# Extra TensorE matmuls with unread results in the drain and between the experts, and one group's slot products moved later

## The chip, the core and the metric

The kernel runs on one core of a Trainium2 chip. The metric is the device time of one execution in microseconds (us); smaller is better. Each execution also has a span, from its first to its last recorded instruction. In the fast executions of this study the time is 1.7 to 2.2 us above the span, mostly 1.8, so a span can be turned into a time by adding about 1.8 us.

## The reference, cut to what matters

Two steps. First a gated recurrence over 5056 positions of 4 sequences, 256 channels wide:

```python
f = lower_bound + (1.0 - lower_bound) * sigmoid(f_logit)
h = f[:, t] * h + (1.0 - f[:, t]) * x[:, t]      # for each t in order
```

Then a soft mixture of experts over all 20224 tokens: 32 slots, 4 for each of 8 experts.

```python
logits = x @ phi                       # 20224 x 32
d = softmax(logits over tokens);  slot_input = d.T @ x
slot_out[e] = relu(slot_input[e] @ w1[e]) @ w2[e]     # w1: 256x1024, w2: 1024x256
out = softmax(logits over slots) @ slot_out
```

No slot input is complete before the last token is scanned, and no output row can be written before the slot outputs are complete. So the kernel has three stages: loading and scanning, a short middle that is mostly matmuls (the drain of the last group, then the experts), and writing the output.

Of the kernel before, what the change touches and what calls it, by code (L numbers as in the profile page):

```python
# [18 lines left out]
def kernel(  # L19
# [10 lines left out]
    nc = tc.nc  # L30
# [5 lines left out]
    P = 128  # L36
# [3 lines left out]
    G = P * R  # L40
    n_grp = (S + G - 1) // G
    n_unit = n_grp * B
# [58 lines left out]
    w1_sb = [store.tile([P, DC, F], BF16, name=f"w1_sb{e}") for e in range(E)]  # L101
    w2_sb = [store.tile([P, FC, D], BF16, name=f"w2_sb{e}") for e in range(E)]

    def load_w(i):
        if i < E:
            nc.gpsimd.dma_start(out=w1_sb[i], in_=w1_r[i])
        else:
            k = FC // 2 if i == 2 * E - 1 else FC
            for c in range(0, FC, k):
                nc.gpsimd.dma_start(out=w2_sb[i - E][:, ds(c, k)],  # L110
                                    in_=w2_r[i - E][:, ds(c, k)])


    W_AT = {12: 1, 18: 1, 24: 1, 30: 1, 34: 3, 35: 1, 36: 8}
    w_next = [0]
# [5 lines left out]
    with tc.tile_pool(name="ld", bufs=3) as ld, \  # L121
# [141 lines left out]
        def row_sums(g):  # L263
            n_p = rows(g)
            ew = etall[:, ds(g * G, n_p * R)].rearrange("s (p r) -> s p r", r=R)
            for r in range(R):
                nc.tensor.matmul(rs_ps[:n_p, g, r], ew[:, :, r], ones,
                                 start=True, stop=True, skip_group_check=True)

        def slots(g):  # L270
            n_p = rows(g)
            et, ht = ets.pop(g), hts.pop(g)
            for r in range(R):
                for b in range(B):
                    nc.tensor.matmul(slot_ps[ds(b * NS, NS), :], et[:n_p, r, b],  # L275
                                     ht[:n_p, b, r],
                                     start=(g == 0 and r == 0),
                                     stop=(g == n_grp - 1 and r == R - 1),
                                     skip_group_check=True)

        def unit(f, m):
            if 0 <= m < n_unit:
                f(m)
# [19 lines left out]
        def late_weights(bs, copy):  # L303
            k, w = ds(bs[0] * NS, len(bs) * NS), len(bs) * NS
            ew = etall[k, ds(last * G, G)].rearrange("s (p r) -> s p r", r=R)
            if bs[0] == 0:
                ets[last] = etok.tile([P, R, B, NS], BF16, name="et", tag="et")
            for r in range(R):
                nc.tensor.transpose(late_ps[:, r, k], ew[:, :, r], ident[k, k])
            copy(ets[last][:, :, ds(bs[0], len(bs))].rearrange("p r b s -> p r (b s)"),  # L310
                 late_ps[:, :, k])

        def late_slots(bs):
            for r in range(R):
                for b in bs:
                    nc.tensor.matmul(slot_ps[ds(b * NS, NS), :], ets[last][:, r, b],
                                     hts[last][:, b, r],
                                     start=False, stop=r == R - 1,
                                     skip_group_check=True)
# [19 lines left out]
        for n in range(n_unit):  # L339
            if n < SINGLE - 2:  # L340
                if n:
                    unit(u_to_channels, n + 1)
                    unit(to_tokens, n - 1)
                s_to_channels(n + 2)
                decay(n + 2, 1)
                if n + 3 < SINGLE:
                    gate(n + 3, 1)
                else:
                    gate(n + 3)
                if n % 2 == 0:  # L350
                    unit(load, n + AHEAD)
                unit(enter, n + 3)
            else:
                if n % 2 == 0:
                    unit(load, n + AHEAD)
                    unit(gate, n + 4)
                else:
                    unit(decay, n + 1)
                if n == 34:
                    exps(7)  # L360
                elif n != 33:
                    group(exps, n - 2)

                unit(enter, n + 3)
                for _ in range(W_AT.get(n, 0)):
                    load_w(w_next[0])
                    w_next[0] += 1

                unit(to_tokens, n - 1)
                if n % 2 == 0:  # L370
                    unit(s_to_channels, n + 2)
                    unit(s_to_channels, n + 3)
                unit(u_to_channels, n + 1)
                group(logits, n - 1)
            if n == n_unit - 1:
                tail = psp.tile([P, 2, G], F32, name="tail", tag="sp")
                rs_ps = tail[:, 0, ds(0, n_grp * R * B)].rearrange(
                    "p (g r b) -> p g r b", r=R, b=B)
                late_ps = tail[:, 1].bitcast(BF16)[:, ds(0, R * P)].rearrange(
                    "p (r s) -> p r s", r=R)  # L380
                logits(last, [0, 1, 2])
                late_exps([0, 1, 2])
                for g in range(4):
                    row_sums(g)

            unit(scan, n)
            if n == 0:
                rep_constants()
            unit(keep_tokens, n - 1)
            if n == 35:  # L390
                weights_to_tokens(7)
            elif n != 34:
                group(weights_to_tokens, n - 3)
            if n == 36:
                slots(6)
            elif n == 37:
                slots(7)
            elif n != 35:
                batch(slots, n - 4, 0)
                batch(slots, n - 4, 1)  # L400
        late_weights([0, 1, 2], nc.scalar.copy)
        logits(last, [3])
        late_exps([3])
        to_tokens(n_unit - 1)
        nc.vector.tensor_copy(hts[last][:, B - 1].rearrange("p r d -> p (r d)").bitcast(F32),
                              hps.pop(n_unit - 1).rearrange("p r c -> p (r c)"))
        late_slots([0, 1, 2])
        late_weights([3], nc.vector.tensor_copy)
        late_slots([3])
        for g in range(4, n_grp):  # L410
            row_sums(g)
# [3 lines left out]
    with tc.tile_pool(name="ew", bufs=1) as ew, \  # L415
# [12 lines left out]
        for o in range(DC):  # L428
            nc.tensor.matmul(sin_ps[:, o], slot_v[:, o], rep2[:, :NS],
                             start=True, stop=True, skip_group_check=True)  # L430
        sin = ew.tile([P, DC, NS], BF16, name="sin")
        for o in range(DC):
            nc.vector.tensor_scalar_mul(sin[:, o], sin_ps[:, o], omlb[:, ds(o, 1)])
# [23 lines left out]
            his.append(hi)  # L457
        cs_ps = pm.tile([P, 1], F32, name="cs_ps", tag="pm")
        nc.tensor.matmul(cs_ps, rep2, cs1, start=True, stop=True)
        for q in range(E // Q):  # L460
            ht_ps = psu.tile([P, FC, P], BF16, name="ht_ps", tag="up")
            hi_v = his[q].rearrange("p (c f) -> p f c", f=FC)
            for fc in range(FC):
                nc.tensor.transpose(ht_ps[:, fc], hi_v[:, fc], ident)

            src = ht_ps.rearrange("p f (j s) -> p f j s", s=NS)[:, :, :, ds(0, SPE)]
            src = bass.AP(tensor=src.tensor, offset=src.offset + q * Q * SPE,
                          ap=[list(src.ap[0]), [P, FC], [NS + SPE, Q], [1, SPE]])
            dst = hid[:, :, ds(q * Q, Q), ds(0, SPE)]
            dst = bass.AP(tensor=dst.tensor, offset=dst.offset + q * Q * SPE,  # L470
                          ap=[list(dst.ap[0]), [E * NS, FC], [NS + SPE, Q], [1, SPE]])
            if q == 0:
                nc.scalar.copy(dst, src)
            else:
                nc.vector.tensor_copy(dst, src)
            for w in range(W):
                e = E - W + w
                if e // Q == q:
                    src = ht_ps[:, :, ds((e % Q) * NS + e * SPE, SPE)]
                    nc.scalar.copy(wide[:, :, w, :, ds(e * SPE, SPE)],  # L480
                                   src.unsqueeze(2).broadcast_to([P, FC, B, SPE]))
# [8 lines left out]
        for e in range(E - W):  # L490
            for fc in range(FC):
                nc.tensor.matmul(so4_ps[ds(fc % 4 * NS, NS), :], hid[:, fc, e],
                                 w2_sb[e][:, fc],
                                 start=(e == 0 and fc < 4),
                                 stop=(e == E - W - 1 and fc >= FC - 4),
                                 skip_group_check=True)
        so4 = ew.tile([P, D], F32, name="so4")
        nc.vector.tensor_copy(so4, so4_ps)
        so_ps = pm.tile([P, D], F32, name="so_ps", tag="pm")
        nc.tensor.matmul(so_ps, rep2, so4, start=True, stop=False, skip_group_check=True)  # L500
        for w in range(W):
            for fc in range(FC):
                nc.tensor.matmul(so_ps, wide[:, fc, w].rearrange("p b s -> p (b s)"),
                                 w2_sb[E - W + w][:, fc],
                                 start=False, stop=w == W - 1 and fc == FC - 1,
                                 skip_group_check=True)
# [73 lines left out]
```

## The kernel before: what the change touches

The tokens are cut into 10 groups of 512 positions times 4 sequences, so there are 40 units; group 9 is the last. In each unit VectorE scans and TensorE transposes. The end of the main loop and the drain, cut:

```python
for n in range(n_unit):
    # ... loads, gates, transposes, logits of earlier groups ...
    if n == n_unit - 1:
        tail = psp.tile([P, 2, G], F32, name="tail", tag="sp")
        # rs_ps is a view of tail[:, 0], late_ps one of tail[:, 1]
        logits(last, [0, 1, 2])
        late_exps([0, 1, 2])
        for g in range(4):
            row_sums(g)
    unit(scan, n)
    unit(keep_tokens, n - 1)
    # ... weights_to_tokens; slot products of the groups 6 and 7 at n = 36, 37 ...
    elif n != 35:
        batch(slots, n - 4, 0)      # at n = 39: group 8
        batch(slots, n - 4, 1)
late_weights([0, 1, 2], nc.scalar.copy)
logits(last, [3])
late_exps([3])
to_tokens(n_unit - 1)
# ... copy ...
late_slots([0, 1, 2])
late_weights([3], nc.vector.tensor_copy)
late_slots([3])
for g in range(4, n_grp):
    row_sums(g)
nc.vector.tensor_copy(slot_sb, slot_ps)
```

The experts, cut. The tile names in the profiles are `sin_ps` (slot inputs), `hi_ps` (first layer), `ht_ps` (hidden, transposed) and `so_ps` (second layer). Six experts go through `hid`; the last two go through `wide`.

```python
sin_ps   = ...  4 matmuls          # slot inputs, then a VectorE multiply
hi_ps    = ... 32 matmuls with w1  # four experts side by side in the array
ht_ps    = ... 2 x 8 transposes
so4_ps   = ... 48 matmuls with w2 of the experts 0 to 5
so_ps    = rep2 x so4              # gathers the six
so_ps   += 16 matmuls, wide x w2 of the experts 6 and 7
slot_out = so_ps * rcs
```

The weights come through GpSimd's DMA queue, converted to bf16, in this order: the eight w1, then the eight w2. The last w2 comes in two halves:

```python
def load_w(i):
    if i < E:
        nc.gpsimd.dma_start(out=w1_sb[i], in_=w1_r[i])
    else:
        k = FC // 2 if i == 2 * E - 1 else FC
        for c in range(0, FC, k):
            nc.gpsimd.dma_start(out=w2_sb[i - E][:, ds(c, k)], in_=w2_r[i - E][:, ds(c, k)])
```

The softmax here doesn't subtract the row's maximum and nothing guards it: scores larger than these inputs give would overflow.

## Time and profile before

| | us |
|---|---|
| time, median of 3 (range) | 209.4 (209.04 to 209.43) |
| the profiled execution: span | 208.8 |
| the profiled execution: time | 210.53 |

From the page of the kernel before: its span, then the granted TensorE clock in tenths of full speed and the busy share of the DMA engines in tenths, in 40 slices of 5.2 us each.

```profile
span 208.8 us, 3060 instructions
...
PEclk9999859999999979997999969586975555555555
DMA  5999999999999999999999999999069999999994
```

DMA is full in nearly every slice but the 29th and 30th (146 to 157 us): the end of the middle stage. The clock falls to 5 tenths in parts of the middle.

The same kernel, busy time of each engine in stretches of 5 us; the last three columns are the granted clock (1.00 is full), the DMA share and GB/s.

```profile
core 0: us, PE busy (x) PEld busy (x) DVE busy (x) ACT busy (x) POOL busy (x), PEclk, DMA share, GB/s
...
130.00:135.00 5.00, 4.77 (x48) 2.24 (x48) 3.34 (x5) 1.16 (x3) 3.58 (x3) 0.55 1.05 212
135.00:140.00 5.00, 4.62 (x53) 3.30 (x52) 1.34 (x3) 0.79 (x2) 0.00 (x0) 0.77 1.07 214
140.00:145.00 5.00, 4.50 (x43) 2.02 (x44) 1.86 (x5) 1.19 (x2) 0.00 (x0) 0.66 1.05 194
145.00:150.00 5.00, 4.46 (x75) 3.64 (x74) 1.76 (x6) 0.70 (x3) 0.00 (x0) 1.00 0.29 54
```

TensorE is busy over 4.4 us of each 5, at a clock of 0.55 to 0.77 until 145 us. DMA, meanwhile, is also full until about 145 us: these are the weights.

The same kernel's TensorE in order of time. The columns are start, duration, engine, line, operation, output and inputs, sizes, count, and in brackets the idle time before and what ended it.

```profile
130.23 0.99 PE L210 MATMUL hp<-ident_f,h 128*128 128x128 f32 x4 [0.90 <-DVE h L199]
131.15 1.04 PE L234 MATMUL lg<-h,phi 128*32 128x512 bf16 x6
...
132.75 1.04 PE L275 MATMUL slot_ps<-ht,et 112*32 112x256 bf16 x16
...
134.16 1.03 PE L234 MATMUL lg<-h,phi 128*32 128x512 bf16 x2
...
138.39 1.22 PE L267 MATMUL tail<-ones,etall 128*128 128x4 bf16 x24
...
140.61 3.53 PE L449 MATMUL hi_ps<-w_sb,sin 128*32 128x512 bf16 x32 [0.50 <-DVE sin L433]
...
148.20 1.91 PE L503 MATMUL so_ps<-w_sb,wide 128*128 128x256 bf16 x16
```

The slot products of group 8 (132.75) stand ahead of the last logits (134.16). The first layer takes 3.53 us, nearly all at half clock. The last 16 matmuls run without a wait.

The same kernel's chain of waits at the end of the middle stage: start, duration, engine, what.

```profile
148.36 1.76 PE so_ps L503 x16
150.15 0.49 DVE slot_out L507
150.68 0.78 PE op L520 x16
```

In this execution no transfer stands in the chain: from 130.2 us on TensorE, with short VectorE steps between, leads to `slot_out`.

### The profile page before, as it was taken

How to read it: one execution, taken by the hardware profiler on the slowest of the kernel's cores; microseconds unless marked ns; L12 is line 12 of the kernel's file. 1: busy time of each engine (PE TensorE's matmuls, PEld its weight loads, DVE VectorE, ACT ScalarE, POOL GpSimd, SP SyncE). 2: the span in 40 equal slices, each digit the busy share in tenths (PEclk: the TensorE clock that was granted, in tenths of full speed). 3: DMA queues.
4: the chain of work that ended last, by engine and by line, in shares of the span. 5: the costliest groups of instructions: out<-in, count | busy, mean ns of one | idle time of the engine just before them, and what ended most of it. 6: DMA issues, size and time to landing. Idle time of an engine off the chain costs nothing.

```text
span 208.8 us, 3060 instructions
## 1 busy us (share of the span) xinstructions
PE 136.6 (65%) x1084; PEld 94.8 (45%) x1084; DVE 146.2 (70%) x160; ACT 133.9 (64%) x180; POOL 98.1 (47%) x66
## 2 busy tenths in 40 slices
PE   0657567675867597747867296989757677877400
PEld 0336445564655475546656285455533233343100
DVE  1677539999999979999799589533385364655520
ACT  3575798899999988899885964302083445456320
POOL 1555669966998396938979892500000000000000
PEclk9999859999999979997999969586975555555555
DMA  5999999999999999999999999999069999999994
GB/s 196 415 412 408 411 410 406 411 411 408 397 321 421 345 384 414 407 318 414 411 345 373 189 213 213 214 213 191 10 249 397 407 407 406 407 407 405 337 376 177
DMA packets 19982, 71.26 MB, mean 341 GB/s; under 512 B 2240, under 2 KB 2240, under 8 KB 19968
## 3 DMA queue, kind: packets, MB, share of 16 engines
q1 hardware_dynamic: 17232, 62.66, 76.0%
q0 software_dynamic: 2448, 8.39, 20.5%
q8 instruction: 8, 0.13, 0.2%
q10 hardware_dynamic: 288, 0.03, 0.1%
q14 instruction: 6, 0.05, 0.1%
HBM read 58.75 MB, written 20.71 MB: 381 GB/s over the span
## 4 chain that ended last, share of the span: by engine, by line
PE 25%; DMA 23%; DVE 22%; ACT 11%; issue 8%; SPq 3%; POOL 3%; DVEq 0%; ACTq 0%; POOLq 0%
DMA out_dram<-ob 13%; DVE h L199 13%; DMA f_t<-in_f_logit_dram 10%; PE hp L210 7%; ACT s_t L151 5%; DVE ob L527 5%; PE sp L167 5%; PE up L167 3%; DVE ht L219 3%; POOL u_t L162 3%; SPq L549 3%; ACT a L189 2%; ACT ob L533 2%; PE lg L234 2%; PE hi_ps L449 2%
## 5 line engine op out<-in xcount | busy, mean ns | idle before, releaser
L162 POOL TENSOR_TENSOR u_t<-s_t,x_t 128x1024 bf16<-128x1024 bf16 x39 | 83.0, 2154 | 26.0 <-ACT s_t L151 23.1
L199 DVE TENSOR_TENSOR_SCAN h<-a,h,up 128x512 bf16<-128x512 f32 (+1 forms) x72 | 86.1, 1249 | 6.4 <-ACT ht L219 3.4
L210 PE MATMUL hp<-ident_f,h 128*128 128x128 f32 (+1 forms) x160 | 32.0, 328 | 31.3 <-DVE ht L219 17.8
L189 ACT ACTIVATE a<-sp,nomlb 128x1024 f32<-128x1024 bf16 (+2 forms) x46 | 43.4, 995 | 11.3 <-PE sp L167 8.7
L527 DVE TENSOR_TENSOR ob<-op,rrow 128x1024 f32<-128x1024 f32 (+2 forms) x25 | 28.9, 1180 | 21.1 <-DMA out_dram<-ob 17.8
L151 ACT ACTIVATE s_t<-f_t 128x2048 bf16<-128x2048 f32 (+1 forms) x23 | 38.8, 1690 | 6.7 <-DMA f_t<-in_f_logit_dram 6.4
L533 ACT ACTIVATE ob<-op,rrow 128x256 f32<-128x256 f32 (+1 forms) x64 | 25.0, 477 | 28.0 <-DVE ob L527 19.3
L210 PEld LDWEIGHTS hp<-ident_f,h 128*128 128x128 f32 (+1 forms) x160 | 23.4, 209 | 41.8 <-DVE ht L219 21.4
L520 PE MATMUL op<-slot_out,etall 32*128 32x256 bf16 (+1 forms) x160 | 33.0, 379 | 12.6 <-ACT ob L533 10.2
L167 PE MATMUL sp<-ident_f,s_t 128*128 128x128 f32 x160 | 26.4, 315 | 9.6 <-ACT s_t L151 8.5
L167 PE MATMUL up<-ident_f,u_t 128*128 128x128 f32 x160 | 26.6, 292 | 4.2 <-POOL u_t L162 4.1
L520 PEld LDWEIGHTS <-etall 32*128 32x128 bf16 (+1 forms) x160 | 15.2, 130 | 30.3 <-issue 25.9
L167 PEld LDWEIGHTS sp<-ident_f,s_t 128*128 128x128 f32 x160 | 22.5, 167 | 11.0 <-issue 5.8
L167 PEld LDWEIGHTS up<-ident_f,u_t 128*128 128x128 f32 x160 | 20.1, 151 | 6.3 <-POOL u_t L162 5.5
L219 DVE COPY ht<-hp 128x512 f32<-128x512 f32 (+1 forms) x20 | 13.5, 674 | 6.7 <-PE hp L210 6.7
L219 ACT COPY ht<-hp 128x512 f32<-128x512 f32 (+1 forms) x19 | 11.1, 582 | 4.3 <-PE hp L210 4.3
L199 DVE TENSOR_TENSOR_SCAN h<-a,up 128x512 bf16<-128x512 f32 x8 | 9.2, 1205 | 1.2 <-PE up L167 1.2
L234 PE MATMUL lg<-h,phi 128*32 128x512 bf16 (+1 forms) x80 | 8.1, 431 | 0.0
L275 PE MATMUL slot_ps<-ht,et 128*32 128x256 bf16 (+1 forms) x144 | 6.7, 315 | 0.0
L110 POOL DMA_DIRECT2D w_sb<-in_moe_w_dram x9 | 4.8, 558 | 3.7 <-DMA w_sb<-in_moe_w_dram 3.7
L151 ACT ACT_TABLE_LOAD x4 | 5.1, 1283 | 1.7 <-PEq L564 1.7
L454 ACT ACTIVATE hi<-hi_ps 128x512 bf16<-128x512 f32 x2 | 1.2, 597 | 6.8 <-issue 5.7
(62 smaller groups left out, 72.2 us busy)
## 6 DMA issues: line engine op xcount, KB each, us to landing
x_t<-in_x_dram SPq DMA_DIRECT2D x40, 512.0 KB, 10.2
f_t<-in_f_logit_dram SPq DMA_DIRECT2D x17, 1024.0 KB, 12.0
out_dram<-ob SPq DMA_DIRECT2D x34, 512.0 KB, 6.0
w_sb<-in_moe_w_dram POOLq DMA_DIRECT2D x15, 512.0 KB, 9.0
f_t<-in_f_logit_dram SPq DMA_DIRECT2D x6, 512.0 KB, 7.9
out_dram<-ob SPq DMA_DIRECT2D x4, 448.0 KB, 6.5
out_dram<-ob SPq DMA_DIRECT2D x4, 256.0 KB, 2.3
w_sb<-in_moe_w_dram POOLq DMA_DIRECT2D x2, 256.0 KB, 19.4
```

Source lines behind the costliest of these rows:

```text
L151: nc.scalar.activation(sts[n // 2][:, ds(n % 2, k)], fs[n // 2][:, ds(n % 2, k)], ACT.Sigmoid, scale=-1.0)
L162: nc.gpsimd.tensor_tensor(uts[n], s_t, x_t, ALU.mult)
L167: nc.tensor.transpose(ps[:, :, r], t[:, r], ident_f)
L189: nc.scalar.activation(decays[n // 2, o][:, ds(n % 2, k), :T], sp[:, ds(n % 2, k), :T, o], ACT.Identity, scale=nomlb[:, ds(o, 1)], bias=1.0)
L199: nc.vector.tensor_tensor_scan(h[:, :T, o], decays[n // 2, o][:, n % 2, :T], up[:, :T, o], hs[n - B][:, ds(used(n // B - 1) - 1, 1), o] if ...
L210: nc.tensor.transpose(hp[:n_p, r], hw[:, :n_p, r], ident_f)
L219: copy(hts[g][:n_p, b].rearrange("p r d -> p (r d)").bitcast(F32), hps.pop(n)[:n_p].rearrange("p r c -> p (r c)"))
L234: nc.tensor.matmul(lg[ds(b * NS, NS), :], phi[:, o], hs[g * B + b][:, :T, o], start=o == 0, stop=o == DC - 1, skip_group_check=True)
L275: nc.tensor.matmul(slot_ps[ds(b * NS, NS), :], et[:n_p, r, b], ht[:n_p, b, r], start=(g == 0 and r == 0), stop=(g == n_grp - 1 and r == R ...
L520: nc.tensor.matmul(op[:n_p, r], ew[ds(b * NS, NS), :, r], slot_out[ds(b * NS, NS), :], start=True, stop=True, skip_group_check=True)
L527: nc.vector.tensor_tensor(ob[:n_p, ds(r, k)], op[:n_p, ds(r, k)], rrow[:n_p, g, ds(r, k), ds(b, 1)].broadcast_to([n_p, k, D]), ALU.mult)
L533: nc.scalar.activation(ob[:n_p, r], op[:n_p, r], ACT.Copy, scale=rrow[:n_p, g, r, ds(b, 1)])
```

## The change

The intent is to keep TensorE's clock up. The change puts matmuls whose results nobody reads ("spins", 128x512, bf16) where TensorE is thought to wait, and puts useful work, group 8's slot products, into the wait after the last logits. There are 27 spins. The diff, with the unchanged lines cut:

```diff
+    def spin(dst, k):
+        for _ in range(k):
+            nc.tensor.matmul(dst, w1_sb[0][:, 0, :P], w1_sb[0][:, 0, :G],
+                             start=True, stop=True, skip_group_check=True)
 ...
                 for g in range(4):
                     row_sums(g)
-
+                late_weights([0, 1, 2], nc.scalar.copy)
+                spin(lgs[0][:, ds(G, G)], 2)
+
+            if n in (n_unit - 3, n_unit - 2):
+                spin(lgs[0][:, ds(G, G)], 3)
             unit(scan, n)
 ...
-            elif n != 35:
+            elif n != 35 and n != n_unit - 1:
                 batch(slots, n - 4, 0)
                 batch(slots, n - 4, 1)
-        late_weights([0, 1, 2], nc.scalar.copy)
         logits(last, [3])
 ...
-        late_slots([0, 1, 2])
+        late_slots([0, 1])
         late_weights([3], nc.vector.tensor_copy)
+        slots(last - 1)
+        late_slots([2])
         late_slots([3])
 ... after the slot inputs:
+        spin(tail[:, 1], 3)
 ... ahead of the hidden transposes, and after each of their two halves:
+        spin(tail[:, 1], 2)
+            spin(tail[:, 1], 2)
 ... after the second layer of the experts 0 to 5:
+        spin(tail[:, 1], 2)
 ... ahead of the second layer of the experts 6 and 7:
+        spin(tail[:, 1], 8)
```

## The prediction

> **What bounds the kernel now.** By the page's slices and the busy-by-stretch view: loading and scanning (0 to 127 us, DMA share near 1.0), the drain and experts (127 to 152 us), the output (152 to 209 us, DMA share 1.0, about 405 GB/s). The change acts in the middle one. There the chain of waits runs almost wholly through TensorE from 130.2 to 150.1 us, whose waits are short: 0.9, 0.7, 0.6, 0.5, 0.5 and 0.4 us. By the clock record TensorE is at 0.5 from 130.5 to 137.3 and from 140.7 to 144.1 us, else at 1.0.
>
> [...] all changes lie whole multiples of 3.41 us apart.[...]
>
> **What it costs and gives.** 27 extra 128x512 matmuls; from the first-layer products (0.85 us for eight, four at a time, at half clock) I estimate 0.43 us each at half and 0.22 at full clock.
> - 3+3 before the scans of units 37 and 38 fill idle time at 126.5 and delay the last weight transposes by 0.65 us, to about when VectorE is ready for its copy (130.0). If they hold the clock, the half-clock stretch 130.5 to 137.3 goes.
> - Group 8's 16 slot matmuls (1.04 us) leave the path ahead of the last logits and fill the wait for the last weights' copy (0.4 us idle). Two spins (0.4 to 0.85) take their old place.[...]
> - First layer: 3.5 us at half, about 1.8 at full clock.
> - Against it: the spins around the hidden transposes stand where TensorE did not wait (about 1.3 us), and the eight before the last two experts cost 1.7 us.
>
> **What limits the gain.** The weight queue. By the packets of the software queue the last half of the last weight lands at 147.9 us; its four matmuls (0.119 us each) can end at 148.5 at best, against 150.1 now: at most 1.6 us can be won. All at full clock, I get the eight spins ending about 147.3 and the last expert at 149.2: gain 0.9 us. If the clock still falls at 137.3[...], half-clock spins make it about 0.5 us slower. The output is bound by DMA, so either passes one to one to the end.
>
> **Prediction: 208.7 us, 80% range 207.9 to 209.6.** Faster by over 2%: 1%. Within 2%: 98%. Slower: 1%.
>
> **What would show it.** Clock record: 1.0 from 124 past 134 us; the dip at 141 to 144 gone or shorter. Timeline: last logits about 133 instead of 134.2; late row sums starting about 136 instead of 138.4; first layer 1.8 to 2.5 us; second layer starting before 145; eight spins of 1.7 us; slot_out 0.5 to 1.5 us earlier; weight queue's end near 147.9; still 58 us from slot_out to the end.
>
> **What would make it wrong.**[...] the early spins delaying the copy before the last scans; the end of weight DMA moving; the output stage changing with another clock at its start.

The cuts marked above take out what no trace or run of this case showed: premises on when the clock changes, a risk that rested on them, and one term of the sum, counted against the change, for splitting the late slot products. The sum itself came to a gain of 0.9 us: eight spins ending at about 147.3 us and the last expert at 149.2, against 150.1 in the profile of before. As one of its terms is cut, the terms that are left need not add up to it.

## The result, and the profile after

| | before | after |
|---|---|---|
| time, median of 4 (range) | 209.42 (209.04 to 209.45) | 209.67 (209.53 to 209.99) |
| ratio after / before, 95% interval | | 1.0018 (1.0001 to 1.0036) |
| profiled execution: span | 208.8 | 207.8 |
| profiled execution: time | 210.53 | 209.61 |
| profiled execution: `slot_out` written | 150.6 | 149.7 |
| from there to the end | 58.1 | 58.1 |

A ratio is the mean time of one kernel's fast runs over that of the other's of the same rounds, so it is not quite the ratio of the medians quoted beside it.

The table holds a contradiction to be explained. By the profiles the change saves 1.0 us of span. By the times it saves nothing and costs about 0.2%.

The page of the changed kernel: span, clock, DMA.

```profile
span 207.8 us, 3114 instructions
...
PEclk9999658889996999999799999999965555555555
DMA  5999999999999999999999899999269999999994
```

The changed kernel in the same stretches.

```profile
core 0: us, PE busy (x) PEld busy (x) DVE busy (x) ACT busy (x) POOL busy (x), PEclk, DMA share, GB/s
...
130.00:135.00 5.00, 4.82 (x70) 2.89 (x70) 3.56 (x5) 1.95 (x5) 4.09 (x3) 1.00 1.07 215
135.00:140.00 5.00, 5.00 (x73) 3.10 (x69) 2.17 (x6) 1.19 (x2) 0.00 (x0) 1.00 1.06 212
140.00:145.00 5.00, 5.00 (x75) 3.18 (x74) 1.96 (x7) 0.70 (x3) 0.00 (x0) 1.00 1.06 203
145.00:150.00 5.00, 3.77 (x32) 2.35 (x33) 0.48 (x1) 0.00 (x0) 0.00 (x0) 1.00 0.40 70
```

The clock is full through the whole middle, as intended. TensorE of the changed kernel in order of time; L116 is the line of the spins.

```profile
129.92 0.63 PE L239 MATMUL lg<-h,phi 128*32 128x512 bf16 x6
...
132.06 0.63 PE L239 MATMUL lg<-h,phi 128*32 128x512 bf16 x2
...
135.15 1.23 PE L272 MATMUL tail<-ones,etall 128*128 128x4 bf16 x24
...
137.46 1.91 PE L460 MATMUL hi_ps<-w_sb,sin 128*32 128x512 bf16 x32
...
144.62 1.89 PE L116 MATMUL tail<-w_sb 128*128 128x512 bf16 x8
146.35 1.61 PE L518 MATMUL so_ps<-w_sb,wide 128*128 128x256 bf16 x12
148.61 0.60 PE L518 MATMUL so_ps<-w_sb,wide 128*128 128x256 bf16 x4 [0.65 <-DMA w_sb<-in_moe_w_dram]
```

The row sums start 3.2 us earlier than in the profile before (135.15 against 138.39), and the first layer takes 1.91 us, not 3.53. Then eight spins run, and after them the last four matmuls wait for the last half of the last weight. The chain of waits now passes through that transfer:

```profile
130.05 18.52 DMA w_sb<-in_moe_w_dram
148.57 0.04 issue
148.61 0.61 PE so_ps L518 x4
149.25 0.49 DVE slot_out L522
```

So 3.2 us won in the drain and 1.6 us in the first layer are 0.9 us at `slot_out` (150.63 to 149.73). The rest went into spins and into that wait. It remains to find where the 0.9 us went in the timed runs.

### The profile page after: what moved, and what is told of

Read it like the earlier page. It is cut to its first block, busy times and chain, and to the rows that moved or that the text cites. A ratio compares the mean times of both kernels' runs of the same rounds, so it can differ in the third digit from the quotient of the medians.

```text
span 207.8 us, 3114 instructions
## 1 busy us (share of the span) xinstructions
PE 141.8 (68%) x1111; PEld 97.8 (47%) x1111; DVE 146.3 (70%) x160; ACT 133.4 (64%) x180; POOL 98.0 (47%) x66
## 4 chain that ended last, share of the span: by engine, by line
DMA 38%; DVE 20%; PE 15%; ACT 11%; issue 8%; POOL 2%; SPq 2%; DVEq 0%; ACTq 0%; POOLq 0%
DMA out_dram<-ob 16%; DMA w_sb<-in_moe_w_dram 13%; DVE h L204 12%; DMA f_t<-in_f_logit_dram 6%; ACT s_t L156 5%; PE hp L215 5%; PE sp L172 5%; DVE ob L542 4%; ACT a L194 4%; DVE ht L224 3%; PE up L172 3%; DMA x_t<-in_x_dram 2%; ACT ob L548 2%; POOL u_t L167 1%; SPq L564 1%
## 5 line engine op out<-in xcount | busy, mean ns | idle before, releaser
L535 PE MATMUL op<-slot_out,etall 32*128 32x256 bf16 (+1 forms) x160 | 34.0, 387 | 11.9 <-ACT ob L548 10.2
L172 PE MATMUL sp<-ident_f,s_t 128*128 128x128 f32 x160 | 27.2, 321 | 9.3 <-ACT s_t L156 8.2
L172 PE MATMUL up<-ident_f,u_t 128*128 128x128 f32 x160 | 27.6, 300 | 4.1 <-POOL u_t L167 4.0
L172 PEld LDWEIGHTS up<-ident_f,u_t 128*128 128x128 f32 x160 | 21.0, 156 | 6.2 <-POOL u_t L167 5.4
L239 PE MATMUL lg<-h,phi 128*32 128x512 bf16 (+1 forms) x80 | 7.5, 420 | 0.0
L280 PE MATMUL slot_ps<-ht,et 128*32 128x256 bf16 (+1 forms) x144 | 6.0, 289 | 0.0
```

Source lines behind the costliest of these rows:

```text
L172: nc.tensor.transpose(ps[:, :, r], t[:, r], ident_f)
L239: nc.tensor.matmul(lg[ds(b * NS, NS), :], phi[:, o], hs[g * B + b][:, :T, o], start=o == 0, stop=o == DC - 1, skip_group_check=True)
L280: nc.tensor.matmul(slot_ps[ds(b * NS, NS), :], et[:n_p, r, b], ht[:n_p, b, r], start=(g == 0 and r == 0), stop=(g == n_grp - 1 and r == R ...
L535: nc.tensor.matmul(op[:n_p, r], ew[ds(b * NS, NS), :, r], slot_out[ds(b * NS, NS), :], start=True, stop=True, skip_group_check=True)
```

## The experiments

Three theories. **A**: the weight queue bounds the middle stage of both kernels in ordinary executions. The profile of before was an untypical execution, whose clock fell in bad places, so the gain that the two profiles show is not there on average. **B**: that profile was typical, and the change wins about 1 us in the drain and loses it elsewhere. **C**: the spins themselves cost time, whatever the queue does.

All kernels of one job ran on one chip and share its runs of the kernel before. On the three chips of these jobs executions spread more than in the first comparison: on each, the 11 runs of before range over 2.4 to 3.3 us. So single medians mean little, and an interval is about half a per cent to either side. The differences between means of two kernels of one job quoted below are uncertain by 0.7 to 1.1 us (95%, from the scatter of their runs). A run more than 1.5% above the fastest of its kernel is counted as slow and left out of means and ratios: one run of e2, and two of the unchanged kernel in the third job (210.66 and 210.79 us). What tells theories apart is mostly inside the profiles, and the larger differences between kernels of one job.

### First job: the kernel before again, and the parts of the change

**e1_before_again**: no edit.

> The kernel before, unchanged, for a second profile and for spans of ordinary executions. Theory A (the profile of before was untypical: it took 210.53 us where the timed runs took 209.04 to 209.45, and the changed kernel's spans are 1.8 us under its times, so the ordinary span of before should be near 207.6): spans of these runs 207.3 to 207.9, and a profile with more of the drain at full clock, slot_out written at about 149.0 to 149.4 us. Rival B (the profile of before was typical and the change wins about 1 us in the drain and loses it elsewhere): spans near 208.8, slot_out near 150.1. Ratio to before 1.000 either way.

Measured: ratio 1.0012 (0.9962 to 1.0061); spans 206.8 to 209.2, four of six between 207.2 and 208.6. The profiled execution took 209.11 us, span 207.3. TensorE in it, from the first layer on:

```profile
138.69 2.50 PE L449 MATMUL hi_ps<-w_sb,sin 128*32 128x512 bf16 x32 [0.50 <-DVE sin L433]
...
145.93 1.47 PE L503 MATMUL so_ps<-w_sb,wide 128*128 128x256 bf16 x12
147.84 0.60 PE L503 MATMUL so_ps<-w_sb,wide 128*128 128x256 bf16 x4 [0.44 <-DMA w_sb<-in_moe_w_dram]
```

And from its chain of waits:

```profile
148.48 0.49 DVE slot_out L507
```

The unchanged kernel reaches its last experts at 145.9 instead of 148.2 us, and waits for the same weight as the changed one. By the clock record the only dip between 123 and 150 us is from 139.9 to 143.3 us; in the first profile there were two, from 130.5 to 137.3 and from 140.7 to 144.1. `slot_out` is written at 148.96 us, 1.7 us earlier than in the first profile and 0.8 us earlier than in the changed kernel's. The profile that the prediction was read from is thus one end of a range. Of the 37 fast executions of the unchanged kernel on the three chips (31 as the reference, 6 of this run) three took 210.53 us or more, one of them with the very time, span and clock of the first profile, so perhaps that execution counted once more; the median span is 207.5, with it or without. My bound of 207.9 for all spans was too narrow: executions spread more than I expected. Not all of that spread need lie in the drain: over the fourteen profiles the stretch from `slot_out` to the end is 57.4 to 58.7 us long.

**e2_no_eight**: the changed kernel without the eight spins.

```diff
-        spin(tail[:, 1], 8)
```

> The changed kernel without its eight spins before the last two experts. If the landing of the last weight bounds the drain (theory A; in the profile after, the last four products waited 0.65 us for it), the time stays within 0.3 us of the changed kernel and the wait grows to about 1.1 us or more (12 products need 1.4 us). If the spins lie on the path (rival B), it is about 1.2 to 1.9 us faster: near 208.

Measured: ratio to before 0.9968 (0.9919 to 1.0017). The changed kernel wasn't in this job, so its time could not be compared directly here. The profile has full clock, and waits in place of the spins:

```profile
146.20 1.03 PE L517 MATMUL so_ps<-w_sb,wide 128*128 128x256 bf16 x8 [1.08 <-DMA w_sb<-in_moe_w_dram]
147.69 0.60 PE L517 MATMUL so_ps<-w_sb,wide 128*128 128x256 bf16 x4 [0.45 <-DMA w_sb<-in_moe_w_dram]
148.94 0.60 PE L517 MATMUL so_ps<-w_sb,wide 128*128 128x256 bf16 x4 [0.65 <-DMA w_sb<-in_moe_w_dram]
```

The last experts wait 2.2 us in three pieces (1.08, 0.45 and 0.65), one for each transfer still on its way. In this execution the queue bounds the stage; TensorE doesn't.

**e3_reorder_only**: all 27 spins taken out, the reordering kept.

```diff
-                spin(lgs[0][:, ds(G, G)], 2)
-            if n in (n_unit - 3, n_unit - 2):
-                spin(lgs[0][:, ds(G, G)], 3)
 ... and every spin(tail[:, 1], ...)
```

> The reordering of group 8's slot products and of the late weights, without any of the 27 spins. Theory A: within 0.4 us of before, clock dips somewhere in the drain as in the profile of before. Rival B, where the spins themselves cost: faster than the changed kernel by about 1 us.

Measured: 0.9997 (0.9954 to 1.0041). By the clock record the dips are there (131.8 to 135.2 and 138.6 to 142.0 us), the first layer takes 3.36 us, and still the last four matmuls wait 1.14 us for the weight. Even with two dips there was time to lose.

**e4_spins_only**: the spins kept, the order of before restored.

```diff
-        late_slots([0, 1])
-        late_weights([3], nc.vector.tensor_copy)
-        slots(last - 1)
-        late_slots([2])
+        late_slots([0, 1, 2])
+        late_weights([3], nc.vector.tensor_copy)
         late_slots([3])
 ... late_weights([0, 1, 2]) and its two spins behind group 8's slot products
```

> The 27 spins at the same places, the slot products and late weights in the order of before. Theory A: within 0.4 us of the changed kernel, clock at full from about 124 us to 150 us, the last products waiting for the last weight. Rival B: slower than the changed kernel by 0.5 to 1 us since the reordering hid group 8.

Measured: 1.0057 (1.0008 to 1.0105); I expected full clock, and missed. In the profile the clock fell from 137.9 to 141.3 us all the same:

```profile
137.82 1.45 PE L116 MATMUL tail<-w_sb 128*128 128x512 bf16 x3
...
148.94 1.91 PE L516 MATMUL so_ps<-w_sb,wide 128*128 128x256 bf16 x16
```

Three spins took 1.45 us here, against 0.81 us in the changed kernel. The last experts began only at 148.9, after the last packet of the weight had ended at 147.8. In this execution the spins lay on the path, and `slot_out` came at 151.4 us. So the spins did not hold the clock in this execution, and the three at its fall took 1.8 times as long. Whether the order makes the difference to the changed kernel was not settled: the two were not on one chip.

### Second job: the floor taken away

The floor is the earliest time at which the weight queue lets the last experts end. If the queue hides the saving, it must come out when the queue ends sooner. In three kernels the last two w2 are not loaded, and the last two experts use the sixth's. Their outputs are wrong, which doesn't matter for the times.

```diff
     def load_w(i):
+        if i >= 2 * E - 2:
+            return
 ...
-                                 w2_sb[E - W + w][:, fc],
+                                 w2_sb[E - W - 1][:, fc],
```

**e5_after_again**: the changed kernel, no edit.

> The changed kernel once more, for a second profile[...] and on a chip shared with the kernels below. Theory A (weight queue bounds the drain of both kernels): ratio to before 0.998 to 1.005, slot_out written within 0.5 us of 149.7, and the last four products of the last expert waiting for the weight unless a dip of the clock let them come late. Rival C (the spins themselves make it slower, whatever the queue): ratio over 1.004 with the last products not waiting.

Measured: 1.0029 (0.9987 to 1.0071), mean 209.39 us against 208.82 of before. In the profile the first layer took 1.91 us and the eight spins 1.89 us, the same as at full clock in the first profile of the changed kernel; the last twelve and four products run nearly without a gap (`slot_out` at 148.9). In this execution the eight spins and the transfer ended almost together; the profile shows a wait of about 0.1 us, where theory A allowed so little only for a clock dip. `slot_out` also lies 0.8 us from the 149.7 expected, outside my 0.5.

**e6_before_no_floor**: before, with the edit above.

> Kernel before with the floor taken away: the last two second-layer weights are not loaded, and the last two experts use the sixth's (wrong result on purpose), so the queue ends about 5 us earlier, near 143. Theory A: TensorE alone bounds this drain; slot_out at 148.0 to 150.6[...], at most 1 us earlier than before.

Measured: 0.9972 (0.9924 to 1.0020), mean 208.19 us. The profile is of the luckiest of its runs (span 204.7; the six spans run to 207.4):

```profile
138.08 1.91 PE L451 MATMUL hi_ps<-w_sb,sin 128*32 128x512 bf16 x32 [0.50 <-DVE sin L435]
...
144.05 1.91 PE L505 MATMUL so_ps<-w_sb,wide 128*128 128x256 bf16 x16
```

By the clock record this execution had full clock from 122.6 to 149.9 us, without a single spin. `slot_out` came at 146.5 us, 1.5 us before what I had expected as the best. So the unchanged kernel's spans still spread over 2.7 us when the last weights no longer bound it.

**e7_after_no_floor**: the changed kernel with that edit.

> The changed kernel with the same two weights left out (wrong result on purpose). Theory A: the eight spins now lie on the path, wide products run without a wait from about 146.4 to 148.3, slot_out at about 149.0; so 0.3 to 0.8 us faster than the changed kernel, near the kernel before with the floor removed (within 0.7 us of it).

Measured: 1.0024 (0.9983 to 1.0064), mean 209.26 us: only 0.1 us faster than e5, against the 0.3 to 0.8 expected, and 1.1 us slower than e6, where I had expected them within 0.7. On average the spins alone bring TensorE to the last experts about as late as the weight lands.

```profile
145.68 1.89 PE L118 MATMUL tail<-w_sb 128*128 128x512 bf16 x8
147.41 1.91 PE L520 MATMUL so_ps<-w_sb,wide 128*128 128x256 bf16 x16
```

**e8_no_eight_no_floor**: that edit, and the eight spins taken out.

> The changed kernel without the eight spins and without the last two weights (wrong result on purpose). Theory A: 1.7 us faster than the one with the eight spins and the floor removed, slot_out at about 147.2, so about 2 us faster than the unchanged kernel: the drain's saving that the weight queue hides. Rival B or C (the spins cost what they save): no faster than the kernel before with the floor removed.

Measured: 0.9890 (0.9851 to 0.9928), mean 206.46 us.

```profile
144.75 0.70 PE L516 MATMUL so_ps<-so,rep 128*128 128x256 f32 x2 [0.21 <-DVE so L514]
145.28 1.91 PE L519 MATMUL so_ps<-w_sb,wide 128*128 128x256 bf16 x16
```

This is the test that decides. Without the floor, the reordering and the other 19 spins together are worth 1.7 us (206.46 against 208.19 of e6, give or take 1 us), so rival B falls: the drain's saving is real and is not lost elsewhere. Rival C holds for the eight spins, which cost time without any queue. Which part of the 1.7 us is the order's and which the spins' was not separated, and single profiles don't show it: e6's lucky one has `slot_out` at 146.5 us, e8's at 147.7. The eight spins cost 2.8 us there (209.26 against 206.46). That is more than the 1.7 us they take in the profile. The two means carry an uncertainty of about 0.7 us, and e7's profiled execution had also ended its scans 0.5 us later, so I don't read a further mechanism into the difference.

### Third job: how much the eight cost with all weights loaded

**e9_after_third**: the changed kernel, no edit.

> The changed kernel on the same chip as the three below, so that they are compared with it directly. Theory A: ratio to before 0.999 to 1.005.

Measured: 1.0014 (0.9954 to 1.0073), mean 209.48 us. In its profile nothing waits for the weight: its last packet ended at 146.6 us, and the eight spins lie on the chain.

```profile
144.34 1.89 PE L116 MATMUL tail<-w_sb 128*128 128x512 bf16 x8
146.06 1.91 PE L518 MATMUL so_ps<-w_sb,wide 128*128 128x256 bf16 x16
```

So of the three profiles of the changed kernel one waits 0.65 us for the weight, one about 0.1 us (e5) and one not at all. For the changed kernel theory A does not hold as I stated it: in two of three executions its own spins, and not the queue, set the end.

**e10_no_eight_again**: the edit of e2.

> The changed kernel without its eight spins, again, beside the changed kernel. Theory A: the last weight's landing takes their place, so 0 to 0.7 us faster than the changed kernel; the last four products wait for the weight. If the eight spins lay wholly on the path: 1.7 us faster.

Measured: 0.9978 (0.9922 to 1.0035), mean 208.74 us, so 0.74 us under the changed kernel, just outside my range of 0 to 0.7. The difference is uncertain by 1.0 us, so it isn't clear of noise. In the profile the second of the last two experts waits 0.97 us for the first half of its weight, and about 0.3 us more for the second. By the means the eight spins are paid in part, with less than half of their 1.7 us; the interval allows anything from nothing to all.

**e11_sixteen**: sixteen instead of eight.

```diff
-        spin(tail[:, 1], 8)
+        spin(tail[:, 1], 16)
```

> Sixteen spins instead of eight before the last two experts. Theory A: the first eight fill a wait, so the next eight (8 x 0.216 = 1.73 us) are paid in full but for the rest of the wait (0.1 to 0.65 us): 1.1 to 1.7 us slower than the changed kernel, and no wait for the weight in the profile. If spins were harmless: no change.

Measured: 1.0077 (1.0024 to 1.0130), mean 210.81 us: 1.3 us slower than the changed kernel. Eight more spins take 1.73 us, so by the means what is not paid is 0.4 us.

```profile
144.89 3.62 PE L116 MATMUL tail<-w_sb 128*128 128x512 bf16 x16
148.34 1.91 PE L518 MATMUL so_ps<-w_sb,wide 128*128 128x256 bf16 x16
```

With no, eight and sixteen spins the means are 208.74, 209.48 and 210.81 us. Theory A reads this as the first eight partly hidden under the landing of the weight and the next hardly. But the steps of 0.74 and 1.33 us are each uncertain by about 1 us, so only their sum, 2.1 us for sixteen spins, is clear of noise.

**e12_drain_spins**: only the 11 spins of the drain and the slot inputs kept.

```diff
-        spin(tail[:, 1], 2)
-            spin(tail[:, 1], 2)
-        spin(tail[:, 1], 2)
-        spin(tail[:, 1], 8)
```

> The changed kernel with the 11 spins of the drain and of the slot inputs only (3, 3, 2 and 3), without the sixteen around the hidden transposes and the second layer. Theory A: TensorE reaches the last experts 2.5 to 3 us sooner than in the changed kernel, and waits for the weights there: within 0.4 us of the kernel without the eight. Candidate for the best version; I expect 0.2 to 0.8 us faster than before, within the noise of 2%.

Measured: 1.0004 (0.9949 to 1.0059), mean 209.29 us. It isn't better; it was expected within 0.4 us of e10 and is 0.55 us above, inside the spread. In the profile TensorE came early, waited for the weights, and the clock fell from 145.5 to 148.9 us.

```profile
145.26 2.56 PE L514 MATMUL so_ps<-w_sb,wide 128*128 128x256 bf16 x12 [1.16 <-DMA w_sb<-in_moe_w_dram]
148.05 0.98 PE L514 MATMUL so_ps<-w_sb,wide 128*128 128x256 bf16 x4 [0.24 <-DMA w_sb<-in_moe_w_dram]
```

The last four took 0.98 us instead of 0.60. Why the clock fell was not shown: TensorE was busy about 1.6 us of the 3.4 before the fall, but in e2, waiting for the weights, it was busy about 1.9 of 3.4 (145.8 to 149.2 us) and the clock stayed full.

The only candidate for a version better than both is the changed kernel without the eight spins. It ran twice, with ratios 0.9968 and 0.9978, and both intervals contain 1. I call it no worse, and not shown to be better than before.

## Why the prediction was wrong

The prediction said 208.7 us, with 207.9 to 209.6; measured were 209.67. It missed by 1.0 us and lay outside its range by 0.07. The text doesn't say how its gain of 0.9 us became 208.7, which is 0.7 below the median. Point by point:

- *The clock.* Right. It is full from 101 to 152 us in the profile after.
- *The drain and the first layer.* Right: last logits at 132.1 ("about 133"), late row sums at 135.2 ("about 136"), first layer 1.91 us ("1.8 to 2.5"), second layer at 141.9 ("before 145"), eight spins of 1.73 us. The last experts followed them at 146.35, a full microsecond before the "about 147.3" of the forecast.
- *The limit.* Right in kind: the last four products wait 0.65 us for the last weight. But the landing moves: the last packet ended at 147.9 us in the profile before, at 148.3 in the one after (where the wait ended at 148.6), and at 146.6 to 148.6 in the others with all weights. The form "weight queue's end near 147.9" was too stiff. And the wait ends only some 0.3 us after the last packet (0.8 in e3), which the "148.5 at best" left out.
- *The size at `slot_out`.* Right as a difference of two profiles, 0.9 us forecast and 0.9 found, but by two errors that cancel: TensorE came 1 us earlier than forecast, and the weight later.
- *From `slot_out` to the end.* Right: 58.1 us in both.
- **The step that failed: "its four matmuls (0.119 us each) can end at 148.5 at best, against 150.1 now", and the 0.9 us of gain reckoned from it.** "Now" was one execution of 210.53 us, and I took the gain away from a median of 209.4 us, which belongs to other executions. Taken from its own execution it gives 210.53 - 0.9 = 209.6 us, beside the 209.67 measured; the agreement is close, but it was luck of the same sort, as it joins one profile to a median. In place of that step the runs showed this: a profiled execution of before with `slot_out` at 148.96 us (e1), already waiting for the weight; and a median of 37 executions at a span of 207.5, not 208.8. The room that I gave the change was mostly not there on average. The eight spins, placed to fill a wait for the weight, then stood on the path in two of the changed kernel's three profiles.

What the change does, on average, as sums of what was measured. Without the floor the order and 19 spins give 1.7 us (e8 against e6). With the weights in place only about 0.6 us of it is left (e2 and e10 against before: 0.77 and 0.46 us between the means). The eight spins take back about 0.7 us (e9 against e10). That leaves about 0.1 us of loss; the three comparisons of the changed kernel with before say 0.18%, 0.29% and 0.14%, or 0.3 to 0.6 us (with the two slow runs of before counted, the third would be about zero). Each term has an uncertainty of some 0.5 to 1 us, so the sum agrees but doesn't prove the parts to a tenth.

What stays open: why some executions have their clock dips at 130 to 137 us and others none. The dips of before begin at 130.5 us in one profile and at 139.9 in another, and are 3.4 or 6.8 us long. What sets their place was not shown, so its share in the spread of 3.6 us (207.47 to 211.02) is argued and not shown; over the 37 executions the mean clock and the span are hardly correlated (-0.18), as the mean covers the whole span and not the middle. All that is in question here is small: 1.7 us of 209, or 0.8%, with the floor away, order included.

## What to carry to other kernels

Before reckoning a gain from a profile, put the profiled execution's own time beside the timed ones: where it lies a whole gain above their median, its waits are not the typical ones, and a second profile is worth more than a closer look at the first. Where two resources end within a microsecond of each other (here TensorE and the weight queue), speeding up one is worth only the gap to the other (here 1.7 us without the floor, about 0.6 with it), and padding sized to fill that gap is on the path in an execution in which the gap is smaller (as in e9, where no product waited for the weight). To learn whether a saving is hidden or not there at all, take the other resource away for one run, even with a wrong result.

## What else the traces showed

- Transposes and the clock. In the profile of before TensorE ran nothing but transposes (in the trace, matmuls with an identity) from 120.3 to 123.7 us, at half clock, and from 123.7 to 130.5 us the clock was full; it also stayed full from 79.3 to 86.1 us with transposes alone.
- Busy time and the clock. In the profile of before TensorE was busy 1.82 of 3.41 us at full clock from 127.1 to 130.5 us, and half clock followed; it was busy 1.75 of 3.42 us at full clock from 82.7 to 86.1 us, and the clock stayed full. In the output stage, busy 7.85 of 10 us (180 to 190), the clock stayed at half; and it was busy throughout from 130.5 to 133.9 us at half clock, which lasted to 137.3. Busy time, as the profile counts it, doesn't by itself tell these cases apart.
- Weight loads. The 16 row-sum pairs (128 columns loaded, 4 columns streamed) took 0.69 us at half clock (before, 132.1 us) and 0.69 us at full clock (e1, 132.0 us): 43 ns each in both.
- Instruction fetches. The instruction queue's packets of 16 KB took 0.89 to 1.1 us each in the profile of before, two of them in the weights' last 15 us (at 133.9 and 146.2 us). Whether they delay the weights was not tested.
